# A longer schedule for the softmax denominators' round trip, with two buffers, in an attention and MLP kernel

## The chip, the cores and the metric

The kernel runs on one core of one Trainium2 chip. The metric is the device time of that core in microseconds (us), the median of several runs. Five units work side by side: TensorE (PE, matmuls), VectorE (DVE), ScalarE (ACT), GpSimd (POOL) and the DMA queues (SP, SyncE, issues most of them). Each engine runs its own program in order and waits on semaphores for the others.

## The reference

Layer-normalised x goes two ways, through attention with 32 heads over a cache of 2048 keys, and through a two-layer MLP with squared ReLU; the two are multiplied and added to x. Biases and casts are as in the code; everything comes in as bf16.

```python
xn = layernorm(x)                                    # x: 1 x 2048 x 512
q = (xn @ wq) split into 32 heads of 128
p = softmax(q @ k_cache^T * 128**-0.5)               # per head 2048 x 2048
s = (p @ v_cache), heads side by side, @ wo          # 1 x 2048 x 512
h = xn @ w1 + b1;  h = max(h, 0)**2                  # 1 x 2048 x 1792
g = silu(h @ w2 + b2)
out = x + s * g
```

## The kernel before

The kernel works in 4 blocks of 512 queries. A block with a head is one unit g, so there are 4 x 32 = 128 of them (called heads below). A head has 16 tiles of 128 keys, taken as 8 pairs; a pair is one **step** of the schedule, 1024 steps in all. In a step TensorE makes the scores of one pair (two matmuls into psA), ScalarE takes the exponential of the pair into pT (128 keys x 2 x 512 queries, 8 such buffers), and TensorE multiplies the pair of two steps before (LAG) with V. The remaining matmuls (projections of q, the MLP, the product with wo) are filled in between, two or so in a step, through two banks psF.

The product with V is made in one of two ways, chosen head by head while the program is emitted:

- An **A head** has pT stationary and V moving: 64 matmuls of 129 columns. V has a column of ones, so the denominators come out of the same matmuls. VectorE copies the result (o_un) and takes the reciprocal, GpSimd multiplies, and a DMA transposes the head into oT.
- A **B head** has V stationary and pT moving: 16 matmuls of 512 columns. The result stands transposed already; ScalarE copies it to one of three buffers o_col. The denominators are sums over the keys, which lie on partitions here, so other engines have to make them.

```python
NSL, NSW, NQS, NPT, NOT, NOC, NHS = 3, 4, 3, 8, 3 * HC, 3, 3     # buffers: pT 8, o_col 3, h_sum 3
# ... cut: gen_pv_b, after the last pair of a B head
t_free[b] = t_col[m] = E(
    AC, partial(_act, out=o_col[:, m % NOC, :], in_=bankO(b), func=ACT.Copy),
    deps=[t_PV[pi], t_scale[m - NOC] if m >= NOC else None])
```

A B head's denominators go through these stages. den_part: for each pair, VectorE sums pT over 32-key blocks with a transposing reduction, either the whole pair at once (1024 columns), or GpSimd first adds the pair's halves (part_add into h_sum) and VectorE reduces 512 columns (part_half). den_sum: VectorE adds the pairs' results. den_write and den_read: GpSimd's queue writes d_sum to a scratch in memory and reads it back, so that each group of 32 partitions gets all four groups' sums (d_quad). den_total, den_recip, den_spread: VectorE adds the four, takes the reciprocal and spreads it to 128 x 512 (r_all). den_scale: GpSimd multiplies o_col by r_all into oT.

```python
def den_sum(g):
    m = b_no[g]
    t_sum[m] = E(DV, partial(_reduce, out=d_sum[:], ...),
                 deps=t_parts[g] + [t_dw[m - 1] if m else None])
    pool_calm(now[0], partial(den_write, g))

def den_write(g):
    # ... cut
    t_dw[m] = S.emit_dma(GP, partial(_dma, out=dst, in_=d_sum[:]), sl_dw,
                         deps=[t_sum[m], t_dr[m - 1] if m else None])
    clock["POOL"] = max(clock["POOL"], clock["PE"]) + 560
    pool_calm(now[0] + 3, partial(den_read, g))

def den_read(g):
    # ... cut
    t_dr[m] = S.emit_dma(GP, partial(_dma, out=d_quad[:]..., in_=src), sl_dr,
                         deps=[t_dw[m], t_tot[m - 1] if m else None])
    clock["POOL"] = max(clock["POOL"], clock["PE"]) + 560
    calm(now[0] + 4, now[0] + 7, partial(den_total, g), partial(den_recip, g),
         partial(den_spread, g))
```

Two queues hold what is still to be emitted. `pool_calm(step, f)` puts f into GpSimd's program at that step or later; `calm(ready, due, f...)` puts f into VectorE's program once ready, when VectorE's estimated backlog allows it (ROOM, in ns), or at step due in any case. `clock` is that estimate. GpSimd takes a pair for part_add while its own estimated backlog is below POOL_ROOM. Whether a head becomes B is decided by VectorE's estimated backlog together with what is still owed to it:

```python
choose(g, FIRST_B <= g < NG - 3 and owed(pi) < OWED)
# ... cut
def owed(step):
    return max(clock["DVE"] - clock["PE"], 0) + sum(
        WEIGHT.get(f.func, 500) for x in quiet if x[0] <= step + NPR for f in x[2])
```

Of the kernel before, what the change touches and what calls it, by code (L numbers as in the profile page):

```python
# [9 lines left out]
F32 = mybir.dt.float32  # L10
P = 128
# [216 lines left out]
def bass_recurrent_scan__mha_block_cached__dense_activation_squared_relu__prompt_kernel(  # L228
# [22 lines left out]
    NPR = NKT // 2  # L251
# [9 lines left out]
    CH.append([(0, HC), (HC, 2 * HC), (2 * HC, H)])  # L261
    LAG = 2
    ROOM = 700
    POOL_ROOM = 300
    FIRST_B = 3
    OWED = 6000
    VW = 136

    S = _Sched()
# [13 lines left out]
    def E(eng, fn, deps=(), inc=True):  # L283
        if eng is PE:
            clock["PE"] += free_size(fn.keywords["out"]) / 2.4 + 2.5
        elif eng is DV:
            n = max(free_size(fn.keywords[k]) for k in ("out", "in_") if k in fn.keywords)
            clock["DVE"] = max(clock["DVE"], clock["PE"]) + n / 0.96 + 75
        elif eng is GP:
            n = free_size(fn.keywords["out"])  # L290
            clock["POOL"] = max(clock["POOL"], clock["PE"]) + n * 2.2 + 140
        return S.emit(eng, fn, deps=deps, inc=inc)
# [20 lines left out]
    o_bf = sb("o_bf", [P, 2, TPB, Dh], BF16)  # L313
    NBK = QB // 32
    d_part = sb("d_part", [P, 2, 2 * NPR, NBK], F32)
    d_sum = sb("d_sum", [P, NBK], F32)
    d_quad = sb("d_quad", [P, 4, NBK], F32)
    d_rec = sb("d_rec", [P, NBK], F32)
    r_all = sb("r_all", [P, NBK, 32], F32)
    d_scr = nc.dram_tensor("d_scr", [32, 4 * NBK], F32, kind="Internal").ap()  # L320
    r_t = sb("r_t", [P, 2, QB], BF16)
    z_t = sb("z_t", [P, 2, D], F32)
    th_t = sb("th_t", [P, 1, D], BF16)
# [22 lines left out]
    def bankF(i):  # L346
        return psF[:, i * 512:(i + 1) * 512]
# [17 lines left out]
    sl_xt = [S.slot(f"xt{i}") for i in range(TPB)]  # L365
    sl_out = [S.slot("out0"), S.slot("out1")]
    sl_fin = [S.slot("fin0"), S.slot("fin1")]
    sl_dw = S.slot("dw")
    sl_dr = S.slot("dr")

    b_no = {}
    a_no = {}
# [322 lines left out]

    def den_sum(g):
        m = b_no[g]
        t_sum[m] = E(DV, partial(_reduce, out=d_sum[:],
                                 in_=d_part[:, m % 2, 0:len(t_parts[g]), :].rearrange(
                                     "p n b -> p b n")),  # L700
                     deps=t_parts[g] + [t_dw[m - 1] if m else None])
        pool_calm(now[0], partial(den_write, g))

    def den_write(g):
        m = b_no[g]
        dst = bass.AP(tensor=d_scr.tensor, offset=d_scr.offset,
                      ap=[[NBK, 4], [4 * NBK, 32], [1, NBK]])
        t_dw[m] = S.emit_dma(GP, partial(_dma, out=dst, in_=d_sum[:]), sl_dw,
                             deps=[t_sum[m], t_dr[m - 1] if m else None])
        clock["POOL"] = max(clock["POOL"], clock["PE"]) + 560  # L710
        pool_calm(now[0] + 3, partial(den_read, g))

    def den_read(g):
        m = b_no[g]
        src = bass.AP(tensor=d_scr.tensor, offset=d_scr.offset,
                      ap=[[0, 4], [4 * NBK, 32], [1, 4 * NBK]])
        t_dr[m] = S.emit_dma(GP, partial(_dma, out=d_quad[:].rearrange("p a b -> p (a b)"),
                                         in_=src), sl_dr,
                             deps=[t_dw[m], t_tot[m - 1] if m else None])
        clock["POOL"] = max(clock["POOL"], clock["PE"]) + 560  # L720
        calm(now[0] + 4, now[0] + 7, partial(den_total, g), partial(den_recip, g),
             partial(den_spread, g))

    def den_total(g):
        m = b_no[g]
        t_tot[m] = E(DV, partial(_reduce, out=d_rec[:], in_=d_quad[:].rearrange("p a b -> p b a")),
                     deps=[t_dr[m], t_spr[m - 1] if m else None])

    def den_recip(g):
        m = b_no[g]  # L730
        t_rec[m] = E(DV, partial(_recip, out=d_rec[:], in_=d_rec[:]), deps=[t_tot[m]])

    def den_spread(g):
        m = b_no[g]
        base = d_rec[:]
        spread = bass.AP(tensor=base.tensor, offset=base.offset,
                         ap=[list(base.ap[0]), [1, NBK], [0, 32]])
        t_spr[m] = E(DV, partial(_transpose32, out=r_all[:], in_=spread),
                     deps=[t_rec[m], t_scale[m - 1] if m else None])
        pool_calm(now[0], partial(den_scale, g))  # L740

    def den_scale(g):
        m = b_no[g]
# [12 lines left out]
    def calm(ready, due, *fns):  # L756
        quiet.append([ready, due, [f if isinstance(f, partial) else partial(f) for f in fns]])

    def pool_calm(ready, fn):
        pool_quiet.append((ready, fn))  # L760
# [8 lines left out]
    def may_run(x, step, flush):  # L769
        if not flush and step < x[0]:  # L770
            return False
        fn = x[2][0]
        if fn.func in (acc_gate,):
            return fn.args[0] * TPB + fn.args[1] in t_g
        if fn.func in (den_sum, den_total, den_spread):
            m = b_no[fn.args[0]]
            if fn.func is den_sum:
                return tiles[fn.args[0]] == NPR and (m == 0 or m - 1 in t_dw)
            return m == 0 or m - 1 in {den_total: t_spr, den_spread: t_scale}[fn.func]
        return True  # L780

    def owed(step):
# [2 lines left out]

    def pool_may(fn):
        m = b_no[fn.args[0]] if fn.func in (den_write, den_read) else 0
        return m == 0 or m - 1 in {den_write: t_dr, den_read: t_tot}[fn.func]

    def fill_pool(step, flush=False):  # L790
        for x in list(pool_quiet):
# [80 lines left out]
    def norm_recip(g):  # L872
        m = a_no[g]
        t_rden[m] = E(DV, partial(_recip, out=rden[:, m % 2, :], in_=o_un[:, :, Dh]),
                      deps=[t_oev[g][0], t_oev[g][1], t_norm.get(m - 2)])
        pool_calm(now[0], partial(norm_scale, g))

    def norm_scale(g):
        m = a_no[g]
# [57 lines left out]
    def job_h(j, c):  # L937
        js = slice(j % 2 * QB, (j % 2 + 1) * QB)
        box = [None]

        def mm(n, bank):
            box[0] = E(PE, partial(_mm, out=bankF(bank), lhsT=w1_sb[:, n, c * P:(c + 1) * P],
                                   rhs=xnT[:, n, js], start=(n == 0), stop=(n == NDC - 1)),
                       deps=[tok_w1[c // 2], t_bankF[bank]] + tok_xT[j], inc=(n == NDC - 1))
            if n == NDC - 1:
                t_xuse[j] = box[0]
                n_xuse[j] += 1

        def evac(bank, step):
            s = c % 2  # L950
            assert j * NFC + c < 2 or divmod(j * NFC + c - 2, NFC) in t_h2
            t1 = E(DV, partial(_ts, out=r_t[:, s, :], in0=bankF(bank), scalar1=b1f[:, c:c + 1],
                               scalar2=0.0, op0=ALU.add, op1=ALU.max),
                   deps=[box[0], t_b1[0], t_rt[s]])

            t_h2[j, c] = t_rt[s] = E(
                DV, partial(_stt, out=h2T[:, c, :], in0=bankF(bank), scalar=b1f[:, c:c + 1],
                            in1=r_t[:, s, :], op0=ALU.add, op1=ALU.mult),
                deps=[t1] + [t_o2[j - 1, qt] for qt in range(TPB) if j > 0])
            return t_h2[j, c]  # L960
        return NDC, mm, evac
# [112 lines left out]
    for j in range(NQB):  # L1074
        b = 30 + j * (SPB - 6)
        for c in range(NFC):
            k = b + (SPB * 9 // 256) * c
            jobs.append((k, max(k - 130, 4), job_h(j, c), None))
        for qt in range(TPB):
            k = b + (SPB * 9 // 256) * NFC + (SPB * 28 // 256) * qt  # L1080
            jobs.append((k, k - 130, job_o2(j, qt), None))
        for m, (h0, h1) in enumerate(CH[j]):
            if h1 == H and j == NQB - 1:
                continue
            for qt in range(TPB):
                r = j * SPB + NPR * h1 + (24 if h1 < H else 30)
                jobs.append((r + 20 + 15 * qt, r, job_wo(j, m, qt), (j * H + h0, j * H + h1)))
# [5 lines left out]
    def fill_one(step, force=False):  # L1093
        if cur[0] is None:
            for idx, (key, rel, job, p) in enumerate(jobs):
                if isinstance(p, tuple) and None in tok_oT[p[0]:p[1]]:
                    continue
                if rel <= step or force:
                    cur[0] = [job, 0]
                    cur_proj[0] = None if isinstance(p, tuple) else p  # L1100
                    jobs.pop(idx)
                    break
            else:
                return False
        (n, mm, evac), i = cur[0]
        bank = bank_no[0]
        mm(i, bank)
        if i == n - 1:
            t_bankF[bank] = evac(bank, step)
            bank_no[0] ^= 1  # L1110
            cur[0] = cur_proj[0] = None
        else:
            cur[0][1] = i + 1
        return True
# [235 lines left out]
```

The softmax here doesn't subtract the row's maximum and nothing guards it: scores larger than these inputs give would overflow.

## Time and profile before

The kernel takes 1228.53 us (median of 3 runs, 1227.3 to 1230.93). The profiled execution took 1224.54 us, and the span of its instructions is 1222.7 us.

| engine | busy, us | what it does most |
|---|---|---|
| TensorE | 1217.5 | 7565 matmuls: scores 2032 of 512 columns, B heads 1440 of 512, A heads 2432 of 129, projections, MLP and wo |
| ScalarE | 1081.4 | 1024 exponentials of 1025 ns, 90 copies to o_col of 592 ns |
| VectorE | 1014.0 | 272 reductions of a whole pair, 448 of an added pair, the denominators' small steps, evacuations |
| GpSimd | 836.6 | 448 additions of halves, 90 multiplies into oT, 180 DMA issues of the round trip |

In the groups of the profile, a line names the engine, the operation, what is written and read, the shapes and the number of instructions; after the first bar stand busy time (us) and the mean of one (ns), after the second the idle time just before them and what ended it. In the waits, the three numbers are the total in us, the number of times and the longest. In the windows, each engine has its busy time in us and its number of instructions, in the order PE, PEld (weight loads), DVE, ACT, POOL, and then the granted clock, the DMA engines' share and GB/s. In the chain of waits, a line has its start, its length and what ran. In a view of a tile, durations are smallest/median/largest in ns, and after them the first and the last start in us.

### The profile page before, as it was taken

How to read it: one execution, taken by the hardware profiler on the slowest of the kernel's cores; microseconds unless marked ns; L12 is line 12 of the kernel's file. 1: busy time of each engine (PE TensorE's matmuls, PEld its weight loads, DVE VectorE, ACT ScalarE, POOL GpSimd, SP SyncE). 2: the span in 40 equal slices, each digit the busy share in tenths (PEclk: the TensorE clock that was granted, in tenths of full speed). 3: DMA queues.
4: the chain of work that ended last, by engine and by line, in shares of the span. 5: the costliest groups of instructions: out<-in, count | busy, mean ns of one | idle time of the engine just before them, and what ended most of it. 6: DMA issues, size and time to landing. Idle time of an engine off the chain costs nothing.

```text
span 1222.7 us, 20416 instructions
## 1 busy us (share of the span) xinstructions
PE 1217.5 (100%) x7565; PEld 633.5 (52%) x7565; DVE 1014.0 (83%) x1622; ACT 1081.4 (88%) x1134; POOL 836.6 (68%) x842
## 2 busy tenths in 40 slices
PE   9999999999999999999999999999999999999998
PEld 7555455554555544555554555455555554455555
DVE  4788788789989888878999878977798989778783
ACT  7888988898888998989989889998998989989894
POOL 2566776768767678677767656776677767777771
PEclk9999999999999999999999999999999999999999
DMA  9997987777767776877777776776676777677751
GB/s 220 199 236 159 184 166 147 131 136 143 146 150 144 137 136 133 137 142 138 138 144 162 145 133 128 146 143 129 135 153 140 134 147 145 125 129 154 135 116 32
DMA packets 645091, 177.16 MB, mean 145 GB/s; under 512 B 630696, under 2 KB 642728, under 8 KB 644992
## 3 DMA queue, kind: packets, MB, share of 16 engines
q1 hardware_dynamic: 635696, 167.81, 71.0%
q0 software_dynamic: 8624, 7.78, 3.5%
q8 instruction: 60, 0.98, 0.4%
q14 instruction: 39, 0.32, 0.1%
q10 hardware_dynamic: 672, 0.26, 0.1%
HBM read 99.55 MB, written 2.83 MB: 84 GB/s over the span
## 4 chain that ended last, share of the span: by engine, by line
PE 94%; DVE 3%; DMA 2%; issue 1%; POOL 0%; ACT 0%; ACTq 0%; POOLq 0%; DVEq 0%
PE psA L153 35%; PE psO L153 24%; PE psF L153 24%; PE psO L158 10%; DMA d_quad<-d_scr 2%; DVE d_part L213 1%; DMA d_scr<-d_sum 1%; POOL h_sum L166 0%; PE psA L158 0%; DVE out_t L166 0%; ACT pT L162 0%; DVE z_t L176 0%; DVE r_all L217 0%; DVE h2T L176 0%; PE psO L197 0%
## 5 line engine op out<-in xcount | busy, mean ns | idle before, releaser
L162 ACT ACTIVATE pT<-psA 128x1024 bf16<-128x1024 f32 x1024 | 1037.5, 1025 | 121.8 <-PE psA L153 88.0
L153 PE MATMUL psA<-qt_sb,kT 128*128 128x512 bf16 x2032 | 604.4, 379 | 0.0
L166 POOL TENSOR_TENSOR h_sum<-pT 128x512 f32<-128x512 bf16 x448 | 512.5, 1160 | 63.3 <-ACT pT L162 43.1
L153 PE MATMUL psO<-pT,v_sb 128*128 128x512 bf16 x1440 | 428.3, 379 | 0.0
L213 DVE TRANSPOSE_TENSOR_REDUCE d_part<-pT 128x32 f32<-128x1024 bf16 x272 | 326.9, 1211 | 1.7 <-ACT pT L162 1.4
L213 DVE TRANSPOSE_TENSOR_REDUCE d_part<-h_sum 128x16 f32<-128x512 f32 x448 | 301.7, 684 | 14.1 <-POOL h_sum L166 13.8
L153 PEld LDWEIGHTS psA<-qt_sb,kT 128*128 128x128 bf16 x2032 | 186.3, 98 | 170.3 <-ACT pT L162 2.9
L153 PEld LDWEIGHTS psO<-pT,v_sb 128*128 128x128 bf16 x1440 | 140.5, 98 | 170.3 <-issue 4.4
L158 PEld LDWEIGHTS psO<-v_sb,pT 128*128 128x128 bf16 x2432 | 162.4, 98 | 70.3 <-ACT pT L162 0.6
L158 PE MATMUL psO<-v_sb,pT 128*128 128x129 bf16 x2432 | 187.2, 220 | 0.3 <-ACT pT L162 0.3
L153 PE MATMUL psF<-xnT,wq_sb 128*128 128x512 bf16 (+1 forms) x520 | 168.9, 374 | 0.4 <-DVE h2T L176 0.2
L153 PE MATMUL psF<-wo_all,oT 128*128 128x512 bf16 x480 | 163.7, 379 | 0.5 <-DVE z_t L176 0.4
L221 POOL DMA_DIRECT2D d_scr<-d_sum x90 | 64.7, 719 | 115.0 <-DVE d_sum L209 52.2
L166 POOL TENSOR_TENSOR oT<-o_col,r_all 128x512 bf16<-128x512 f32 x90 | 115.1, 1279 | 36.5 <-DVE r_all L217 35.1
L221 POOL DMA_DIRECT2D d_quad<-d_scr x90 | 63.3, 704 | 74.8 <-DMA d_scr<-d_sum 61.6
L180 DVE CAST qt_sb<-psF 128x512 bf16<-128x512 f32 (+1 forms) x130 | 85.8, 660 | 31.1 <-PE psF L153 30.2
L153 PEld LDWEIGHTS psF<-xnT,wq_sb 128*128 128x128 bf16 x520 | 50.3, 98 | 60.7 <-issue 1.3
L153 PE MATMUL psF<-xnT,w_sb 128*128 128x512 bf16 x224 | 77.1, 379 | 0.0
L153 PEld LDWEIGHTS psF<-wo_all,oT 128*128 128x128 bf16 x480 | 46.9, 98 | 57.6 <-DVE z_t L176 0.9
L153 PE MATMUL psF<-w_sb,h2T 128*128 128x512 bf16 x224 | 73.6, 379 | 0.0
L180 DVE COPY o_un<-psO 128x258 f32<-128x258 f32 x76 | 28.9, 420 | 53.6 <-PE psO L158 53.5
L217 DVE STREAM_TRANSPOSE r_all<-d_rec 128x512 f32<-128x512 f32 x90 | 61.8, 686 | 0.8
(61 smaller groups left out, 529.1 us busy)
## 6 DMA issues: line engine op xcount, KB each, us to landing
v_sb<-in_A_v_cache_dram SPq DMA_DIRECT2D x127, 512.0 KB, 4.9
wq_sb<-in_A_wq_dram SPq DMA_DIRECT2D x127, 128.0 KB, 4.6
wo_all<-in_A_wo_dram SPq DMA_DIRECT2D x4, 1024.0 KB, 8.2
w_sb<-in_B_w_dram SPq DMA_DIRECT2D x14, 256.0 KB, 4.7
d_quad<-d_scr POOLq DMA_DIRECT2D x90, 32.0 KB, 3.7
x_t<-in_A_x_dram POOLq DMA_DIRECT2D x16, 128.0 KB, 3.9
kT<-in_A_k_cache_dram SPq DMA_TRANSPOSE x127, 5.0
x_ln<-in_A_x_dram SPq DMA_DIRECT2D x15, 128.0 KB, 4.0
```

Source lines behind the costliest of these rows:

```text
L153: return e.matmul(out, lhsT, rhs, start=start, stop=stop)
L158: return e.matmul(out, lhsT, rhs, start=start, stop=stop, skip_group_check=True)
L162: return e.activation(out, in_, func, bias=bias, scale=scale)
L166: return e.tensor_tensor(out, in0, in1, op)
L180: return e.tensor_copy(out, in_)
L213: return e.tensor_reduce(out, in_, axis=AX.X, op=ALU.add, apply_transpose=True)
L217: return e.transpose(out, in_)
L221: return e.dma_start(out, in_)
```

## The change

The round trip's lags are made longer: the read follows the write by 5 steps instead of 3, the totals follow the read by 7 (due at 11) instead of 4 (due at 7), the write comes one step and the multiply into oT two steps later, and the A heads' multiply one step later. d_sum, d_quad, d_rec, the scratch and their semaphores are doubled, so that a head waits for the head two before it instead of the one before. GpSimd's two DMA issues are estimated at 720 ns each instead of 560, POOL_ROOM goes from 300 to 700 ns, and OWED from 6000 to 8000 ns, with which the plan has 98 heads with V stationary. The aim is that GpSimd and VectorE no longer stand still for the landing of the trip's DMAs, and that more heads can be of the B kind. Buffers of pT, o_col, h_sum and r_all are as before.

```diff
--- before.py
+++ after.py
@@ -261,9 +261,11 @@
     CH.append([(0, HC), (HC, 2 * HC), (2 * HC, H)])
     LAG = 2
     ROOM = 700
-    POOL_ROOM = 300
+    POOL_ROOM = 700
     FIRST_B = 3
-    OWED = 6000
+    OWED = 8000
+    READ_LAG = 5
+    TOTAL_LAG = 7
     VW = 136
 
     S = _Sched()
@@ -313,11 +315,11 @@
     o_bf = sb("o_bf", [P, 2, TPB, Dh], BF16)
     NBK = QB // 32
     d_part = sb("d_part", [P, 2, 2 * NPR, NBK], F32)
-    d_sum = sb("d_sum", [P, NBK], F32)
-    d_quad = sb("d_quad", [P, 4, NBK], F32)
-    d_rec = sb("d_rec", [P, NBK], F32)
+    d_sum = sb("d_sum", [P, 2, NBK], F32)
+    d_quad = sb("d_quad", [P, 2, 4, NBK], F32)
+    d_rec = sb("d_rec", [P, 2, NBK], F32)
     r_all = sb("r_all", [P, NBK, 32], F32)
-    d_scr = nc.dram_tensor("d_scr", [32, 4 * NBK], F32, kind="Internal").ap()
+    d_scr = nc.dram_tensor("d_scr", [2, 32, 4 * NBK], F32, kind="Internal").ap()
     r_t = sb("r_t", [P, 2, QB], BF16)
     z_t = sb("z_t", [P, 2, D], F32)
     th_t = sb("th_t", [P, 1, D], BF16)
@@ -365,8 +367,8 @@
     sl_xt = [S.slot(f"xt{i}") for i in range(TPB)]
     sl_out = [S.slot("out0"), S.slot("out1")]
     sl_fin = [S.slot("fin0"), S.slot("fin1")]
-    sl_dw = S.slot("dw")
-    sl_dr = S.slot("dr")
+    sl_dw = [S.slot(f"dw{i}") for i in range(2)]
+    sl_dr = [S.slot(f"dr{i}") for i in range(2)]
 
     b_no = {}
     a_no = {}
@@ -695,49 +697,51 @@
 
     def den_sum(g):
         m = b_no[g]
-        t_sum[m] = E(DV, partial(_reduce, out=d_sum[:],
+        t_sum[m] = E(DV, partial(_reduce, out=d_sum[:, m % 2, :],
                                  in_=d_part[:, m % 2, 0:len(t_parts[g]), :].rearrange(
                                      "p n b -> p b n")),
-                     deps=t_parts[g] + [t_dw[m - 1] if m else None])
-        pool_calm(now[0], partial(den_write, g))
+                     deps=t_parts[g] + [t_dw[m - 2] if m >= 2 else None])
+        pool_calm(now[0] + 1, partial(den_write, g))
 
     def den_write(g):
         m = b_no[g]
-        dst = bass.AP(tensor=d_scr.tensor, offset=d_scr.offset,
+        dst = bass.AP(tensor=d_scr.tensor, offset=d_scr.offset + m % 2 * P * NBK,
                       ap=[[NBK, 4], [4 * NBK, 32], [1, NBK]])
-        t_dw[m] = S.emit_dma(GP, partial(_dma, out=dst, in_=d_sum[:]), sl_dw,
-                             deps=[t_sum[m], t_dr[m - 1] if m else None])
-        clock["POOL"] = max(clock["POOL"], clock["PE"]) + 560
-        pool_calm(now[0] + 3, partial(den_read, g))
+        t_dw[m] = S.emit_dma(GP, partial(_dma, out=dst, in_=d_sum[:, m % 2, :]), sl_dw[m % 2],
+                             deps=[t_sum[m], t_dr[m - 2] if m >= 2 else None])
+        clock["POOL"] = max(clock["POOL"], clock["PE"]) + 720
+        pool_calm(now[0] + READ_LAG, partial(den_read, g))
 
     def den_read(g):
         m = b_no[g]
-        src = bass.AP(tensor=d_scr.tensor, offset=d_scr.offset,
+        src = bass.AP(tensor=d_scr.tensor, offset=d_scr.offset + m % 2 * P * NBK,
                       ap=[[0, 4], [4 * NBK, 32], [1, 4 * NBK]])
-        t_dr[m] = S.emit_dma(GP, partial(_dma, out=d_quad[:].rearrange("p a b -> p (a b)"),
-                                         in_=src), sl_dr,
-                             deps=[t_dw[m], t_tot[m - 1] if m else None])
-        clock["POOL"] = max(clock["POOL"], clock["PE"]) + 560
-        calm(now[0] + 4, now[0] + 7, partial(den_total, g), partial(den_recip, g),
-             partial(den_spread, g))
+        t_dr[m] = S.emit_dma(GP, partial(_dma, out=d_quad[:, m % 2].rearrange("p a b -> p (a b)"),
+                                         in_=src), sl_dr[m % 2],
+                             deps=[t_dw[m], t_tot[m - 2] if m >= 2 else None])
+        clock["POOL"] = max(clock["POOL"], clock["PE"]) + 720
+        calm(now[0] + TOTAL_LAG, now[0] + TOTAL_LAG + 4, partial(den_total, g),
+             partial(den_recip, g), partial(den_spread, g))
 
     def den_total(g):
         m = b_no[g]
-        t_tot[m] = E(DV, partial(_reduce, out=d_rec[:], in_=d_quad[:].rearrange("p a b -> p b a")),
-                     deps=[t_dr[m], t_spr[m - 1] if m else None])
+        t_tot[m] = E(DV, partial(_reduce, out=d_rec[:, m % 2, :],
+                                 in_=d_quad[:, m % 2].rearrange("p a b -> p b a")),
+                     deps=[t_dr[m], t_spr.get(m - 2)])
 
     def den_recip(g):
         m = b_no[g]
-        t_rec[m] = E(DV, partial(_recip, out=d_rec[:], in_=d_rec[:]), deps=[t_tot[m]])
+        t_rec[m] = E(DV, partial(_recip, out=d_rec[:, m % 2, :], in_=d_rec[:, m % 2, :]),
+                     deps=[t_tot[m]])
 
     def den_spread(g):
         m = b_no[g]
-        base = d_rec[:]
+        base = d_rec[:, m % 2, :]
         spread = bass.AP(tensor=base.tensor, offset=base.offset,
                          ap=[list(base.ap[0]), [1, NBK], [0, 32]])
         t_spr[m] = E(DV, partial(_transpose32, out=r_all[:], in_=spread),
                      deps=[t_rec[m], t_scale[m - 1] if m else None])
-        pool_calm(now[0], partial(den_scale, g))
+        pool_calm(now[0] + 2, partial(den_scale, g))
 
     def den_scale(g):
         m = b_no[g]
@@ -775,8 +779,10 @@
         if fn.func in (den_sum, den_total, den_spread):
             m = b_no[fn.args[0]]
             if fn.func is den_sum:
-                return tiles[fn.args[0]] == NPR and (m == 0 or m - 1 in t_dw)
-            return m == 0 or m - 1 in {den_total: t_spr, den_spread: t_scale}[fn.func]
+                return tiles[fn.args[0]] == NPR and (m < 2 or m - 2 in t_dw)
+            if fn.func is den_total:
+                return m < 2 or m - 2 in t_spr
+            return m == 0 or m - 1 in t_scale
         return True
 
     def owed(step):
@@ -785,7 +791,7 @@
 
     def pool_may(fn):
         m = b_no[fn.args[0]] if fn.func in (den_write, den_read) else 0
-        return m == 0 or m - 1 in {den_write: t_dr, den_read: t_tot}[fn.func]
+        return m < 2 or m - 2 in {den_write: t_dr, den_read: t_tot}[fn.func]
 
     def fill_pool(step, flush=False):
         for x in list(pool_quiet):
@@ -873,7 +879,7 @@
         m = a_no[g]
         t_rden[m] = E(DV, partial(_recip, out=rden[:, m % 2, :], in_=o_un[:, :, Dh]),
                       deps=[t_oev[g][0], t_oev[g][1], t_norm.get(m - 2)])
-        pool_calm(now[0], partial(norm_scale, g))
+        pool_calm(now[0] + 1, partial(norm_scale, g))
 
     def norm_scale(g):
         m = a_no[g]
@@ -939,6 +945,7 @@
         box = [None]
 
         def mm(n, bank):
+            assert None not in tok_xT[j]
             box[0] = E(PE, partial(_mm, out=bankF(bank), lhsT=w1_sb[:, n, c * P:(c + 1) * P],
                                    rhs=xnT[:, n, js], start=(n == 0), stop=(n == NDC - 1)),
                        deps=[tok_w1[c // 2], t_bankF[bank]] + tok_xT[j], inc=(n == NDC - 1))
@@ -1075,7 +1082,7 @@
         b = 30 + j * (SPB - 6)
         for c in range(NFC):
             k = b + (SPB * 9 // 256) * c
-            jobs.append((k, max(k - 130, 4), job_h(j, c), None))
+            jobs.append((k, max(k - 130, 4), job_h(j, c), (None, j)))
         for qt in range(TPB):
             k = b + (SPB * 9 // 256) * NFC + (SPB * 28 // 256) * qt
             jobs.append((k, k - 130, job_o2(j, qt), None))
@@ -1093,7 +1100,8 @@
     def fill_one(step, force=False):
         if cur[0] is None:
             for idx, (key, rel, job, p) in enumerate(jobs):
-                if isinstance(p, tuple) and None in tok_oT[p[0]:p[1]]:
+                if isinstance(p, tuple) and None in (tok_xT[p[1]] if p[0] is None
+                                                     else tok_oT[p[0]:p[1]]):
                     continue
                 if rel <= step or force:
                     cur[0] = [job, 0]
```

The last hunks keep a job of the MLP's first layer from being taken before its normalised inputs are there.

## The prediction

> **What bounds the kernel now.** I read the page's busy shares first, then busy time by window, the chain of waits, the groups by line, the waits, and last the tiles of the denominators' round trip.
>
> ```profile
> PE 1217.5 (100%) x7565; PEld 633.5 (52%) x7565; DVE 1014.0 (83%) x1622; ACT 1081.4 (88%) x1134; POOL 836.6 (68%) x842
> PEclk9999999999999999999999999999999999999999
> ```
>
> TensorE is busy for all of the span and its clock is full, but a busy TensorE proves little, since matmul ends are modelled. So I look at how closely matmuls follow one another. In the chain of waits, a stretch of matmuls on the same engine shows its pace:
>
> ```profile
> 153.38 0.68 PE psO L158 x12
> ...
> 208.54 0.65 PE psF L153 x3
> ```
>
> Twelve 129-column matmuls of an A head (pT stationary) take 0.68 us, 56.7 ns each; three 512-column ones take 0.65 us, 217 ns each. That is the pace of a stream without gaps. The windows, whose first pair of numbers is the TensorE's busy time, show how rarely the stream breaks:
>
> ```profile
> 80.00:120.00 40.00, 39.75 (x262) 21.06 (x260) 34.24 (x55) 35.43 (x38) 24.51 (x27) 1.00 0.90 187
> 500.00:600.00 100.00, 100.00 (x565) 49.54 (x564) 85.36 (x137) 90.33 (x96) 75.68 (x74) 1.00 0.79 140
> 640.00:680.00 40.00, 39.60 (x241) 20.07 (x239) 34.20 (x56) 35.02 (x37) 28.93 (x29) 1.00 0.78 159
> ```
>
> Only four windows between 40 and 1180 us are not full (80, 120, 640 and 900 us: 0.25 + 0.10 + 0.40 + 0.08 us idle, 0.8 us in all). The chain leaves TensorE for long stretches, 83 to 95 and 647 to 676 us for example, through VectorE and the round trip's two DMAs; but those are the places where TensorE lost a few tenths of a microsecond, and the percentages of the chain (DMA 2%, DVE 3%) must not be taken for time to win. The rest of the span is TensorE streaming. This decides the size of the answer: only fewer matmul columns, or those few tenths, can make the kernel faster.
>
> [...]VectorE stood still 31 times for the round trip's landing, although other reductions were ready. [...]the tile view of the round trip has landings of 2.0 us at the least, 3.0 (write) and 3.7 us (read) in the median and 6.6 us at the most[...].
>
> **The change part by part.**
>
> *Fewer A heads.* Before there were 2432 / 64 = 38 A heads and 90 B heads (V stationary); afterwards 30 and 98. An A head's second product is 64 x 56.7 ns = 3.63 us, a B head's 16 x 217 ns = 3.47 us. Eight heads give 8 x 0.16 = 1.3 us. That is all that the 98 heads can bring: it is 0.1%.
>
> *What the eight heads cost the other engines.* From the groups by line:
>
> ```profile
> L166 POOL TENSOR_TENSOR h_sum<-pT 128x512 f32<-128x512 bf16 x448 | 512.5, 1160 | 63.3 <-ACT pT L162 43.1 <-DVE d_part L213 12.6 <-DVE d_rec L184 3.8
> L213 DVE TRANSPOSE_TENSOR_REDUCE d_part<-pT 128x32 f32<-128x1024 bf16 x272 | 326.9, 1211 | 1.7 <-ACT pT L162 1.4
> L213 DVE TRANSPOSE_TENSOR_REDUCE d_part<-h_sum 128x16 f32<-128x512 f32 x448 | 301.7, 684 | 14.1 <-POOL h_sum L166 13.8
> ...
> L217 DVE STREAM_TRANSPOSE r_all<-d_rec 128x512 f32<-128x512 f32 x90 | 61.8, 686 | 0.8
> L162 ACT ACTIVATE o_col<-psO 128x512 f32<-128x512 f32 x90 | 53.3, 592 | 0.0
> ```
>
> VectorE pays (326.9 + 301.7 + 61.8 + 38.7 + 22.3 + 20.4) / 90 = 8.6 us for a B head (the last three are d_sum and d_rec) and (28.9 + 6.8 + 2.1) / 38 = 1.0 us for an A head: 8 x 7.6 = 61 us more. All of VectorE's rows add up to some 1097 us against 1014 busy, because neighbours overlap in the records, so I take 61 x 1014 / 1097 = 56 us: 1070 us. GpSimd pays (512.5 + 115.1 + 64.7 + 63.3) / 90 = 8.4 us against 1.0: 8 x 7.4 = 59 us more, 896 us. ScalarE: 8 x 0.592 = 4.7 us, 1086 us.
>
> *POOL_ROOM 300 to 700.* GpSimd may run further ahead, so it takes more of a head's eight pairs; now it takes 448 / 90 = 4.98. A pair that it takes costs it 1.16 us and saves VectorE 1.21 - 0.68 = 0.53 us. If the share goes to 5.4 (my guess), that is 98 x 0.42 = 41 pairs: VectorE 1070 - 22 = 1048 us (86%), GpSimd 896 + 48 = 944 us (77%). Neither fills up on the average.
>
> *The lags.* These lines are what the lags and second buffers are for:
>
> ```profile
> POOL d_quad L221 <- DMA d_scr<-d_sum: 61.6, 41, 3.5
> ...
> DVE d_rec L209 <- DMA d_quad<-d_scr: 36.5, 31, 3.3
> POOL oT L166 <- DVE r_all L217: 35.1, 41, 3.2
> ```
>
> A step is 1222.7 / 1024 = 1.19 us. The read's gap goes from 3 to 5 steps (3.6 to 6.0 us against a write's 0.7 us of issue and 3.0 us of landing), the total's from 4 to 7 (4.8 to 8.4 us against 3.7). I expect both DMA waits to fall to under a fifth of their 98 us, and the wait of oT's multiply for r_all (two steps later) likewise. These are waits of engines that don't set the end. Off TensorE's path they are worth nothing; on it, they are behind part of the lost tenths: the chain goes through the round trip ahead of the two breaks at 94 and 676 us. Worth: up to 0.5 us in those gaps, perhaps 1 us with pauses too short for the busy time to show.
>
> Sum of gains: 1.3 + 0.5 to 1 = about 2 us.
>
> **The rivals.** *First: o_col becomes the wait.* The diff leaves o_col at three buffers while the trip grows longer. The first head's walk, by first starts:
>
> ```profile
> L209 DVE TENSOR_REDUCE d_sum<-d_part x90: 325/436/506, 50.2 to 1188.0; 128x16 f32<-128x176 f32 x55, 128x16 f32<-128x160 f32 x17, 128x16 f32<-128x192 f32 x17, 128x16 f32<-128x208 f32 x1
> L217 DVE STREAM_TRANSPOSE r_all<-d_rec x90: 658/698/714, 62.7 to 1194.8; 128x512 f32<-128x512 f32 x90
> L162 ACT ACTIVATE o_col<-psO x90: 592/592/599, 47.8 to 1184.6; 128x512 f32<-128x512 f32 x90
> L166 POOL TENSOR_TENSOR oT<-o_col,r_all x90: 1255/1270/1627, 63.8 to 1195.6; 128x512 bf16<-128x512 f32 x90
> ```
>
> o_col is written at 47.8 us and read from 63.8 to 65.1 us: 17.3 us. The change adds 1 (write) + 2 (read) + 3 (total) + 2 (multiply) = 8 steps, 9.5 us, and takes back the (61.6 + 36.5) / 90 = 1.1 us of waiting that a head had: about 25.7 us. The buffer is wanted again three B heads later. A head takes 1222.7 / 128 = 9.55 us, so that is 28.7 us in a run of four or more B heads, and 38 us when an A head lies between. Before, 90 B heads between some 32 A heads made runs of three; 98 between some 24 make runs of four, so about every fourth head has only 3 us to spare. For this rival: the margin. Against it: the emission refuses a plan in which the multiply comes after that copy, so GpSimd is late by its own backlog at most, and ScalarE has waited 88.0 us for TensorE in all, so a short delay is swallowed. If 25 heads lost 0.4 us each, the kernel would take 1228.5 + 10 - 2 = 1236 us.
>
> *Second: VectorE becomes the bound in places.* OWED 6000 to 8000 lets a backlog of 8 us stand where 6 us stood, and an evacuation of psF then waits behind it; TensorE has two psF banks. For it: at 500 to 600 us VectorE is already busy 85%, and one time in four an A head, its pause, is gone. Against it: its 3.3 us stops for a landing go too, and more pairs move to GpSimd. If TensorE lost 0.4 us (what it lost at 640 to 680 us) at some 15 places, the time would be 1228.5 + 6 - 2 = 1232 us.
>
> *Third: nothing new blocks and all old breaks vanish.* 1228.5 - 1.3 - 2 = 1225 us.
>
> **Range and chances.** The gains come to 2 us; I set some 1 us of new short stalls against them, half for o_col and half for VectorE, and so get 1228.5 - 2 + 1 = 1227.5, which I round down to 1227.3 because the plan as a whole lowers waits. The three runs of before lie within 3.6 us, more than the effect. The low end, 1223, needs every break gone and a lucky run; the high end, 1234, leaves room for one of the first two rivals at about two thirds of its size. A gain over 2% (24.6 us) isn't there to be had, as TensorE streams all the time: 0.01. A loss over 2% needs a stall of ScalarE or VectorE in nearly every B head: 0.02. Within 2%: 0.97.
>
> **What would show it.** Right: A matmuls 1920 and B matmuls 1568; DMA waits of d_quad and d_rec under 20 us together; VectorE at 85 to 88%, GpSimd at 75 to 79%; TensorE windows full. o_col's rival: a wait "ACT o_col <- POOL oT" and ScalarE's waits for TensorE falling below 88 us. VectorE's rival: TensorE waits for qt_sb, r_t or h2T, and windows of TensorE under their length in the middle. I am wrong if the span differs from 1222.7 us by more than about 6 us either way.

## The result

The changed kernel takes 1222.35 us (median of 5 runs, 1222.29 to 1222.38) against 1228.53 us (median of 5, 1224.91 to 1230.93): ratio 0.9951, 95% interval 0.9931 to 0.9971. That is 6.2 us or 0.5%. The spread says as much as the median: the runs of the kernel before lie 6 us apart, those of the changed kernel 0.1 us.

In the profile the two kernels lie only 2.2 us apart (spans 1222.7 and 1220.5 us). The profiled execution of the kernel before took 1224.54 us, 4 us under its median; that of the changed kernel took 1222.32 us, its median. The profile of before shows one of the kernel's best executions, and most of the gain lies outside it.

The page of the changed kernel, busy time by engine and the chain of waits by engine:

```profile
PE 1208.3 (99%) x7047; PEld 616.6 (51%) x7181; DVE 1051.6 (86%) x1694; ACT 1083.9 (89%) x1142; POOL 916.5 (75%) x921
...
PE 98%; issue 1%; DVE 1%; ACT 0%; ACTq 0%; POOL 0%; DVEq 0%; POOLq 0%
```

7181 weight loads are 384 fewer than before, 8 heads at 48 each. 134 matmul records are missing, so TensorE's busy time here is not to be set against that of before. VectorE and GpSimd are busier, 86% and 75%, and the chain no longer leaves TensorE for the round trip, which had 2% of it. The waits (total us, times, longest):

```profile
POOL d_scr L221 <- DVE d_sum L209: 44.2, 34, 3.6
POOL oT L166 <- DVE r_all L217: 41.7, 23, 5.0
...
POOL d_quad L221 <- DMA d_scr<-d_sum: 17.0, 17, 2.0
```

GpSimd's wait for the write's landing went from 61.6 to 17.0 us. VectorE's wait for the read's landing, 36.5 us before, is gone from the list. The multiply's wait for r_all did not fall (35.1 before, 41.7 now). The groups that share the denominators' work:

```profile
L166 POOL TENSOR_TENSOR h_sum<-pT 128x512 f32<-128x512 bf16 x511 | 584.3, 1161 | 92.3 <-ACT pT L162 46.2
...
L213 DVE TRANSPOSE_TENSOR_REDUCE d_part<-h_sum 128x16 f32<-128x512 f32 x511 | 341.0, 682 | 5.4 <-POOL h_sum L166 4.6
L213 DVE TRANSPOSE_TENSOR_REDUCE d_part<-pT 128x32 f32<-128x1024 bf16 x273 | 328.4, 1211 | 2.4 <-ACT pT L162 2.1
```

GpSimd takes 511 / 98 = 5.2 of a head's eight pairs, and VectorE's wait for it fell from 13.8 to 4.6 us. The tile view of o_col (smallest/median/largest ns, first and last start) carries the lengthened trip:

```profile
L162 ACT ACTIVATE o_col<-psO x98: 592/592/593, 47.7 to 1182.0; 128x512 f32<-128x512 f32 x98
L166 POOL TENSOR_TENSOR oT<-o_col,r_all x98: 1255/1272/1348, 73.9 to 1195.1; 128x512 bf16<-128x512 f32 x98
```

The first head's o_col is written at 47.7 and read at 73.9 us, 26.2 us later where it was 16.0. Still no copy to o_col waited: the waits have no such line.

### The profile page after: what moved, and what is told of

The parts are those of the page before. It is cut to its first block, busy times and chain, and to the rows that moved or that the text cites. A ratio compares the mean times of both kernels' runs of the same rounds, so it can differ in the third digit from the quotient of the medians.

```text
span 1220.5 us, 19804 instructions
## 1 busy us (share of the span) xinstructions
PE 1208.3 (99%) x7047; PEld 616.6 (51%) x7181; DVE 1051.6 (86%) x1694; ACT 1083.9 (89%) x1142; POOL 916.5 (75%) x921
## 4 chain that ended last, share of the span: by engine, by line
PE 98%; issue 1%; DVE 1%; ACT 0%; ACTq 0%; POOL 0%; DVEq 0%; POOLq 0%
PE psA L153 36%; PE psO L153 28%; PE psF L153 25%; PE psO L158 9%; ACT pT L162 0%; PE psA L158 0%; ACT o_col L162 0%; PE psF L197 0%; ACTq L135 0%; DVE xnT L180 0%; PE psO L197 0%; DVE r_t L172 0%; DVE h2T L176 0%; DVE qt_sb L180 0%; DVE z_t L176 0%
## 5 line engine op out<-in xcount | busy, mean ns | idle before, releaser
L166 POOL TENSOR_TENSOR h_sum<-pT 128x512 f32<-128x512 bf16 x511 | 584.3, 1161 | 92.3 <-ACT pT L162 46.2
L153 PE MATMUL psA<-qt_sb,kT 128*128 128x512 bf16 x1947 | 586.4, 379 | 4.1
L153 PE MATMUL psO<-pT,v_sb 128*128 128x512 bf16 x1543 | 461.3, 379 | 1.5 <-DVE o_un L180 0.2
L213 DVE TRANSPOSE_TENSOR_REDUCE d_part<-h_sum 128x16 f32<-128x512 f32 x511 | 341.0, 682 | 5.4 <-POOL h_sum L166 4.6
L153 PEld LDWEIGHTS psO<-pT,v_sb 128*128 128x128 bf16 x1568 | 153.0, 98 | 185.8 <-issue 3.5
L166 POOL TENSOR_TENSOR oT<-o_col,r_all 128x512 bf16<-128x512 f32 x98 | 124.8, 1273 | 42.5 <-DVE r_all L217 41.7
L158 PEld LDWEIGHTS psO<-v_sb,pT 128*128 128x128 bf16 x1920 | 128.0, 98 | 55.4 <-ACT pT L162 0.6
L158 PE MATMUL psO<-v_sb,pT 128*128 128x129 bf16 x1920 | 147.8, 220 | 0.5 <-ACT pT L162 0.3
L221 POOL DMA_DIRECT2D d_quad<-d_scr x98 | 69.1, 705 | 17.2 <-DMA d_scr<-d_sum 17.0
L180 DVE COPY o_un<-psO 128x258 f32<-128x258 f32 x60 | 22.8, 421 | 54.9 <-PE psO L158 54.8
```

The lines of the kernel that those rows point to most:

```text
L153: return e.matmul(out, lhsT, rhs, start=start, stop=stop)
L158: return e.matmul(out, lhsT, rhs, start=start, stop=stop, skip_group_check=True)
L166: return e.tensor_tensor(out, in0, in1, op)
L180: return e.tensor_copy(out, in_)
L213: return e.tensor_reduce(out, in_, axis=AX.X, op=ALU.add, apply_transpose=True)
L221: return e.dma_start(out, in_)
```

## The experiments

To see where TensorE lost time, I add up in each trace what lies between two matmuls' starts beyond their pace (216 ns for 512 columns, 57 for 129: the medians from start to start in the profile of before), from 20 to 1195 us, counting what is over 30 ns; where a matmul's record is missing, its weight load shows that it ran, and its pace is taken off. This is called the breaks below. Before: 1.8 us at 8 places. Changed kernel: 0.7 us at 5. The difference of 1.1 us and the 1.3 us worked out for the eight heads make about the 2.2 us between the two profiles. The question is where the other 4 us of the medians come from.

Theory: the short lags let engines stand still for DMAs whose landing time varies, and TensorE loses another amount in each execution. Rival: the eight heads bring more than worked out.

### The kernel before once more, and each half of the change

The first run is the kernel before, unchanged.

> The kernel before, unchanged, to see its spread and a second profile. Landing theory (the short lags make engines stand still for DMAs whose landing time varies, and TensorE loses a different amount in each run): runs spread over 3 us or more between 1224 and 1231 us, and the breaks of TensorE between 40 and 1180 us, 1.8 us in the first profile, come out different in this one, at other places. Heads theory (the 98 heads bring the gain, by more than the 1.3 us of matmul time worked out): the same spread, but it has nothing to do with the gain; the breaks stay near 1.8 us at the same places.

Measured: 1227.95 us, 14 runs from 1224.51 to 1230.33; the 19 runs of the kernel before beside it: 1227.64 us, 1226.0 to 1230.51. The profiled execution was again the fastest. Its breaks come to 1.7 us, but the largest, 0.85 us at 889 us, is in no place where the first profile had one. The chain of waits that led to it (start, length, what):

```profile
874.19 4.79 DMA d_scr<-d_sum
878.99 0.30 issue
879.28 0.70 POOL d_quad L221
879.99 0.02 issue
880.01 1.17 POOL h_sum L166
881.18 0.02 issue
881.20 0.71 DVE d_part L213
...
884.61 2.65 DVE acc L176
887.26 2.34 DVE d_part L213 x3
889.60 0.59 DVE acc L166
890.18 0.05 issue
890.23 0.39 PE psF L153
```

A write took 4.8 us to land. GpSimd stood at the read that waits for it, so the next addition came late, VectorE's reductions piled up behind that, and the evacuation of psF that TensorE needed came last. The landing was not alone in this: acc (L176) took 2.65 us in the chain, where 0.68 us is its median (the last section has more on it). Landings of the write range from 2.0 to 6.3 us in the first profile; where a long one falls differs from run to run.

The second run has the lags and second buffers without the new heads, at 90 heads:

```diff
 (the changed kernel)
-    POOL_ROOM = 700
+    POOL_ROOM = 300
-    OWED = 8000
+    OWED = 7000
-        clock["POOL"] = max(clock["POOL"], clock["PE"]) + 720   # both issues
+        clock["POOL"] = max(clock["POOL"], clock["PE"]) + 560
```

> The change's lags and second buffers alone; POOL_ROOM 300 and the estimates of 560 ns as before, OWED 7000 so that the plan has 90 heads with V stationary as before. Landing theory: 1223.9 us (the change's 1222.35 plus the 1.5 us that eight heads are worth), and all runs within 0.5 us. Heads theory: 1227 us or more, since the eight heads are missing, with the spread of before.

Measured: 1223.37 us (1223.19 to 1223.81), ratio 0.9963 (0.995 to 0.9976) to the kernel before beside it. Breaks 0.5 us at 3 places. GpSimd's wait for the write, 61.6 us before, is now

```profile
POOL d_quad L221 <- DMA d_scr<-d_sum: 18.5, 11, 4.0
```

and VectorE's wait for the read is gone from the list. So 4.3 us and the spread go with the lags, the second buffers and the delays of the write and the multiplies together, without one more head.

The third run has the heads alone:

```diff
 (the kernel before)
-    OWED = 6000
+    OWED = 8000
 # and the last hunks of the change (tok_xT)
```

> The heads alone: lags, single buffers, POOL_ROOM and estimates of before, OWED 8000, which gives 98 heads with V stationary (and the guard that keeps the MLP's jobs behind their inputs). Landing theory: 1227 to 1232 us with a spread of 3 us or more, as the stops for landings are still there and eight more heads have them. Heads theory: about 1223 us.

Measured: 1244.0 us (1243.24 to 1247.38), ratio 1.0136 (1.0121 to 1.0151). Both theories were too low: with the old lags and single buffers the eight heads cost 16 us. Breaks: 25.6 us at 45 places. The chain before the largest, 2.6 us at 1012 us:

```profile
1005.42 1.09 POOL h_sum L166
1006.52 5.20 DMA d_scr<-d_sum
1011.72 0.28 issue
1012.00 0.04 POOL d_quad L221
1012.04 0.69 issue
1012.72 1.17 POOL h_sum L166
...
1013.98 1.03 ACT pT L162
1015.01 0.05 issue
1015.06 0.60 PE psA L153 x2
```

The write landed after 5.2 us; the addition queued behind the read on GpSimd was late, and until it was done its pT buffer was not free, so the exponential could not start, and TensorE had no scores. The waits of this kernel have the step that the kernel before hardly had (0.5 us):

```profile
POOL d_quad L221 <- DMA d_scr<-d_sum: 70.2, 48, 3.7
...
ACT pT L162 <- POOL h_sum L166: 15.3, 16, 3.3
```

The fourth run is the kernel before without the two DMAs. It leaves out the exchange between the groups of partitions, so its denominators are not the true ones:

```diff
-        t_dw[m] = S.emit_dma(GP, partial(_dma, out=dst, in_=d_sum[:]), sl_dw, ...)
+        t_dw[m] = t_sum[m]
-        t_dr[m] = S.emit_dma(GP, partial(_dma, out=d_quad[:]..., in_=src), sl_dr, ...)
+        t_dr[m] = t_quad1      # d_quad set once to a constant at the start
```

> The kernel before with the round trip's two DMAs left out: d_quad is set once to a constant, so the denominators are not the true ones; everything else, 90 heads and the place of every other instruction, stays. Landing theory: 1223.9 us or a little less, all runs within 0.5 us. Heads theory: stays near 1227 to 1228 us. A third view, that the break comes from VectorE's load and not from landings: still 2 us or more of breaks in the middle and a spread of runs of over 1 us.

Measured: 1222.73 us (1222.61 to 1223.55), ratio 0.9959 (0.9948 to 0.9971), breaks 0.15 us. Without landings to wait for, the kernel before loses its spread and 4.9 us. It also has 128 us less of issuing on GpSimd, and no head waits for the transfers of the head before, so it bounds what the trip cost rather than measuring the stops alone; but it and the run of the lags at 90 heads, which issues every DMA, come out 0.6 us apart. The landing theory holds; the heads, with POOL_ROOM and the estimates that go with them, are worth 1223.37 - 1222.35 = 1.0 us once the lags are there, and cost 16 us when they are not.

### Which part of the trip's change

The next four take one part of the change back. First the total's lag, at 98 heads:

```diff
 (the changed kernel)
-    OWED = 8000
+    OWED = 7250
-    TOTAL_LAG = 7
+    TOTAL_LAG = 4            # and due at +7
```

> The changed kernel with the total's lag put back (4 steps, due at 7), the read's lag left at 5; OWED 7250, so that it has 98 heads as the change has. In the kernel with 98 heads and the short lags the largest break of TensorE goes back to GpSimd standing still for the write's landing. GpSimd theory (that stop is the one that costs): 1222 to 1225 us, although VectorE still waits some 30 us for the read's landing. VectorE theory (the stop of VectorE for the read's landing holds up reductions and evacuations, and that is what costs): 1230 us or more.

Measured: 1227.6 us (1225.91 to 1228.21, 12 runs). In between. But its profile has a break of some 3 us that has nothing to do with the round trip, seen in the chain:

```profile
551.76 0.32 DVE xn_t L172
552.08 0.03 DVE d_sum L209
552.11 3.12 DMA xnT<-xn_t
```

The plan had put a job of the MLP's first layer right behind the DMA that transposes its normalised input. Second, the read's lag:

```diff
-    READ_LAG = 5
+    READ_LAG = 3
```

> The changed kernel with the read's lag put back to 3 steps, the total's left at 7; OWED 8000, 98 heads. GpSimd theory: 1228 to 1240 us, as GpSimd waits some 60 us for the write's landing again. VectorE theory: 1222 to 1225 us. If both stops cost, both this and the other run lie between 1225 and 1240 us.

Measured: 1235.8 us (1233.38 to 1237.31), with the same accident (3.1 us). Third, the delays of GpSimd's write and multiplies:

```diff
-        pool_calm(now[0] + 1, partial(den_write, g))
+        pool_calm(now[0], partial(den_write, g))
-        pool_calm(now[0] + 2, partial(den_scale, g))
+        pool_calm(now[0], partial(den_scale, g))
-        pool_calm(now[0] + 1, partial(norm_scale, g))
+        pool_calm(now[0], partial(norm_scale, g))
```

> The changed kernel with GpSimd's write and multiplies put back to the step at which they become ready (no 1, 2 and 1 steps of delay); OWED 7750, 98 heads. Landing theory: 1222 to 1223.5 us, since these waits are for VectorE's short instructions and not for a landing. Rival (the multiply stops GpSimd for r_all, 35 us in all before, and that cost as much as the landings): 1225 us or more, with the wait of oT's multiply for r_all well over the change's 41.7 us.

Measured: 1222.1 us (1222.05 to 1222.13). With the long lags, the delays bring nothing: the multiply's wait for r_all is 51.8 us here and doesn't show in the time. Fourth, the lags with single buffers at 90 heads:

```diff
 (the kernel before)
-        pool_calm(now[0] + 3, partial(den_read, g))
+        pool_calm(now[0] + 5, partial(den_read, g))
-        calm(now[0] + 4, now[0] + 7, partial(den_total, g), ...
+        calm(now[0] + 7, now[0] + 11, partial(den_total, g), ...
 # write +1, multiply +2, A heads' multiply +1, the last hunks (tok_xT); OWED = 7000
```

> The change's lags with the single buffers of before (a head waits for the head just before it); POOL_ROOM 300, estimates 560, OWED 7000, 90 heads, so it compares with the run of the lags alone at 90 heads (1223.4 us). Lags theory (the lags are the whole gain at 90 heads, and the second buffers only make room for them): 1223 to 1225 us. Rival (the second buffers take the stops away): 1226 us or more, with waits of GpSimd's write for the read before it.

Measured: 1233.18 us (1232.93 to 1237.41), ratio 1.0043 (1.0026 to 1.006), 10 us over the lags with two buffers and 5 us over the kernel before. Its waits:

```profile
POOL d_scr L221 <- DMA d_quad<-d_scr: 29.2, 15, 2.9
...
ACT o_col L162 <- POOL oT L166: 6.7, 2, 4.3
```

With one buffer the longer trip of a head holds up the write of the next, the multiplies come late, and here o_col does become a wait: ScalarE stood 6.7 us for it, and TensorE has breaks of 3.6 and 1.6 us at the accumulations of the next A head. More was lost just after the longer break: from 385 to 387 us the windows show a granted clock of 0.50, and 512-column matmuls start 427 ns apart instead of 216; that lasted 3.4 us (the mean granted clock of the execution is 0.999), so by estimate from these numbers 1.7 us more were lost. That the break brought the lower clock is not shown. The profile also holds the accident (3.0 us, with no fall of the clock after it), so not all of the 10 us is the buffers'.

### The two lags apart, without the accident

A guard, called so from here on, keeps jobs of the MLP's first layer 8 steps away from the DMA that brings their input:

```diff
+                if isinstance(p, tuple) and p[0] is None and step < xT_step.get(p[1], -8) + 8:
+                    continue      # xT_step[j]: the step of the last transposing DMA of block j
```

> Read's lag 5, total's lag 4 as in the run before it of this kind, with a guard: no job of the MLP's first layer is taken within 8 steps of the transposing DMA that brings its input, since that plan happened to put such a job right behind the DMA and TensorE stood still 3.2 us for it, which has nothing to do with the round trip. 98 heads. If the stop for the read's landing is small beside it: 1224.0 to 1225.0 us (1227.6 less 3.2, so about 2 us over the change). If the stop of VectorE was itself the cost: still 1226.5 us or more.

Measured: 1222.59 us (1222.44 to 1223.05): the read's lag alone keeps 98 heads within 0.3 us of the change.

> Read's lag 3, total's lag 7, with the same guard; the plan has 97 heads. If GpSimd's stop for the write's landing is the main cost: 1231 to 1234 us (1235.8 less the 3.1 us that TensorE stood for the input in that profile), still 9 us or more over the change. If that run's time came from the accident: 1226 us or less.

Measured: 1235.36 us (1232.08 to 1237.01), 97 heads: the total's lag alone does not. Its waits, and the group of VectorE's reductions of added pairs:

```profile
POOL d_quad L221 <- DMA d_scr<-d_sum: 86.3, 47, 4.9
...
ACT pT L162 <- POOL h_sum L166: 13.5, 12, 3.2
```

```profile
L213 DVE TRANSPOSE_TENSOR_REDUCE d_part<-h_sum 128x16 f32<-128x512 f32 x502 | 338.0, 685 | 38.4 <-POOL h_sum L166 37.7
```

GpSimd stands 86.3 us for the write; VectorE waits 37.7 us for its additions (4.6 in the changed kernel), and ScalarE 13.5 us. VectorE's wait for the read is not in the list, so at these heads it is GpSimd's stop that costs. Breaks come to 14.3 us at 40 places; here too the clock was at half for 3.4 us, from 172.8 us on, behind a break of 2.9 us (mean granted clock 0.998). Next the buffers alone, with short lags (READ_LAG 3, TOTAL_LAG 4, no delays, the guard, 97 heads):

> The second buffers alone with the short lags of before (3 and 4 steps, multiplies at once), POOL_ROOM 700 and the estimates of 720 as in the change, the guard, 97 heads. Landing theory: both stops are back, 1232 to 1240 us. Rival (single buffers made the 1244 us of the 98 heads with the old lags, by waits for the head before): 1222 to 1226 us.

Measured: 1241.19 us (1239.52 to 1244.64). The buffers alone bring little over the 1244 us of single buffers (98 heads, POOL_ROOM 300). The run with one buffer shows what they are for: they let the long lags run.

At the number of heads of the kernel before (POOL_ROOM 300, estimates 560, the guard), the two lags again:

```diff
-    TOTAL_LAG = 7            # the first run; OWED 6250, 91 heads
+    TOTAL_LAG = 4
-    READ_LAG = 5             # the second run; OWED 6250, 90 heads
+    READ_LAG = 3
```

> At the number of heads of the kernel before: read's lag 5, total's lag 4, second buffers, the guard, POOL_ROOM 300 and estimates 560; OWED 6250, 91 heads. If GpSimd's stop for the write's landing is the cause in the kernel before too: 1223 to 1224.5 us and runs within 1 us, although VectorE's stop for the read's landing is left. If both stops share the 4.3 us: 1225 to 1227 us with a spread of over 2 us.

> The same with read's lag 3 and total's lag 7, OWED 6250, 90 heads. GpSimd's stop as the cause: 1227 us or more with a spread of over 2 us, as in the kernel before. If both share: 1225 to 1227 us. If it was VectorE's stop after all: 1223 to 1224.5 us.

Measured: read's lag alone 1224.24 us (1223.6 to 1224.56), total's lag alone 1222.75 us (1222.48 to 1223.36). Each lag alone takes away most of what the kernel before loses, and the forecasts don't decide between the stops: the first lies where GpSimd's stop as the cause was to put it, the second just under what VectorE's was to give. The wait of VectorE in the first run, and two waits of the second:

```profile
DVE d_rec L209 <- DMA d_quad<-d_scr: 14.4, 10, 3.7
```

```profile
POOL d_quad L221 <- DMA d_scr<-d_sum: 73.1, 41, 4.6
...
DVE d_rec L209 <- DMA d_quad<-d_scr: 1.2, 2, 1.0
```

In the second run GpSimd stands longer for the write than in the kernel before (73.1 against 61.6 us), and it costs nothing: breaks 0.18 us, and the time is that of the kernel without the trip. So in this plan GpSimd's stop is not what costs. What is left is VectorE's stop for the read's landing: it is nearly gone in the second run, and in the first it falls from 36.5 to 14.4 us though its own lag is the old one, perhaps because a read that isn't held up by the write goes out on time. This fits, but it is not shown for the kernel before: its break at 889 us began with a stop of GpSimd, both runs here also have the second buffers and the delays, and buffers and delays with the short lags were not run at 90 heads. That GpSimd's stop costs at 97 heads and not at 90 may come from its load, 73 to 75% busy instead of 68%, with more additions queued behind it that VectorE and ScalarE need. The runs differ in heads and in POOL_ROOM; which of the two takes GpSimd's slack was not put apart.

### The guard by itself, and more heads

> The changed kernel with the guard (no job of the MLP's first layer within 8 steps of its input's transposing DMA), OWED 7750, 98 heads: shows what the guard does by itself. The change has no such wait in its profile, so 1222.0 to 1222.8 us if the guard only removes that accident; under 1221.5 us if it brings something of its own, which would then have to come off what the lags were given credit for.

Measured: 1222.11 us (1221.94 to 1222.14), 0.2 us under the change. The guard only takes away an accident that the change's plan happens not to have; the 5 us between the two runs with the read's lag alone are of that plan, of which some 3 us are explained by the input's landing.

The last adds heads: o_col in bf16, so that four buffers fit, OWED 9000, the guard, 102 heads.

> The changed kernel with o_col in bf16 so that four buffers fit where three were, OWED 9000 and the guard: 102 heads with V stationary. If a head is worth 0.19 us and VectorE and GpSimd still have room: 1221.5 us, a little better than the change. If the plan is at its limit of VectorE: 1223 us or more, with new breaks of TensorE behind VectorE's work.

Measured: 1223.27 us (1222.54 to 1223.64), no gain. Its page:

```profile
PE 1208.2 (99%) x6858; PEld 608.1 (50%) x6989; DVE 1084.5 (89%) x1730; ACT 1085.3 (89%) x1146; POOL 926.1 (76%) x939
```

VectorE is at 89%, and the breaks come to 2.4 us at 12 places (0.35 us at 4 in the run with the guard and 98 heads): four heads at 0.16 us bring 0.6 us of matmul time, and the new breaks take more. In this one plan, 102 heads are past what this division of work carries. Nothing tried beats the change by more than 0.3 us.

## Why the prediction was right and wrong

**Right.** TensorE bounds the kernel, and nothing here could win 2%. Eight heads were to bring 1.3 us; with the lags in place they brought 1.0. The loads came out as worked out: VectorE 1051.6 us (1048 predicted), GpSimd 916.5 (944, mostly as its share of pairs is 5.2 and not 5.4), ScalarE 1083.9 (1086). The trip's first head takes 26.2 us from o_col to the multiply's start (24.4 by the sum of steps), and both DMA waits together are 17 us, under the 20 named. The rival of o_col stayed a rival because the buffers of the trip were doubled; with single ones, at 90 heads, it came.

**Wrong.** The step that failed is the worth of the lags: "up to 0.5 us in those gaps, perhaps 1 us with pauses too short for the busy time to show". It measured 4.3 us (lags, buffers and delays at 90 heads, 1227.64 - 1223.37). The mechanism was the one named, stops for landings that reach TensorE by way of late reductions and evacuations; the size came from the wrong place. I took the lost time from one profiled execution and subtracted it from a median that was 4 us longer. That execution had lost 1.8 us in breaks; the median one must have lost more. The two numbers stood side by side before the prediction, 1224.54 and 1228.53 us, and so did the spread of 3.6 us, which I read as noise ("more than the effect"). It was the effect: the same stream of matmuls has next to no spread of its own here, as the 0.1 us of the changed kernel shows. The low end, 1223 us, was to need "a lucky run"; all five runs lie under it. The 1 us of "new short stalls" set against the gain did not appear either, and the medians of the kernel before, 1227.4 to 1228.5 us from one set of runs to the next, hold most of what is left of the error.

Wrong too: the multiply's wait for r_all was to fall and did not, and the delay of the multiplies has no effect on the time.

Not shown: no execution of the kernel before at 1228 us or more was profiled. The two that were, at 1224.54 and 1224.51 us, were the fastest beside their sets of runs, and whether that is chance isn't known. So where its further loss lay is inferred from the runs in which it vanishes (the lags at 90 heads, no trip, total's lag alone), not seen. Also open is which of the two stops costs most in the kernel before.

## What to carry to other kernels

When the profiled execution is faster than the median, or the runs spread by more than the profile has idle time, the profile doesn't hold the loss: look for engines that stand, with ready work behind, for DMAs of varying landing time (2.0 to 6.6 us for the round trip before), and size the stops by taking the DMA or the wait out. The length of a stop doesn't say what it costs: 73 us of GpSimd's stops were free at 90 heads, while the run with 86 us at 97 heads took 13 us more than the changed kernel; the slack of the engine that stands (GpSimd 68% busy in the first, 73% in the second) is the likely reason, not shown. Here the longer lags needed second buffers: with single ones they became a wait for the neighbour (29.2 us of GpSimd's write for the read before it).

## What the runs showed of the hardware

VectorE's product of acc and g_all (L176, 16 in each profile) takes 0.68 us in the median of the profile of before and far longer at times, 2.20 us there and 3.47 us in that of the changed kernel. In the repeated kernel before, VectorE's and GpSimd's timelines have side by side:

```profile
884.53 2.73 DVE L176 SCALAR_TENSOR_TENSOR acc<-acc,g_all 128x512 f32<-128x512 f32 x1
```

```profile
882.11 3.37 POOL L166 TENSOR_TENSOR h_sum<-pT 128x512 f32<-128x512 bf16 x3
885.45 1.26 POOL L166 TENSOR_TENSOR oT<-o_col,r_all 128x512 bf16<-128x512 f32 x1
```

It starts while GpSimd is in the third of these additions and ends 0.5 us after the multiply. In the profiles of the kernel before and the changed kernel, the 13 with no addition or multiply of GpSimd beside them took 0.63 to 0.69 us, the 19 others 0.65 to 3.47 us. All 17 profiles together have 272 of these operations: the 106 with none beside them took 0.63 to 0.69 us, the 166 others up to 3.48 us. So the long ones are all beside work of GpSimd; what makes them long is not shown. This operation stood in the chain ahead of the break at 889 us.

Work that was ready stood behind some of the waits. In the profile of before, at 17 of VectorE's 31 waits for the read's landing the instruction next behind was a reduction whose input had been there for 0.09 to 1.80 us when the wait ended; it started 0.18 us after the one that had waited.
